# Single-pass turns and a new closing order in a one-token attention kernel

## The chip, the cores, the metric

One core of a Trainium2 chip (trn2). The metric is the device time of one execution in microseconds, as a median of several executions. In the profiles PE is TensorE, PEld its weight load, DVE VectorE, ACT ScalarE, POOL GpSimd, and SP the queue that issues the transfers; the granted clock is the share of full speed that TensorE was allowed. Ratios are computed as the mean time of one kernel's fast runs over the mean of the other's fast runs of the same rounds, so they are not quite the ratio of the medians quoted.

## The reference

One token attends to 16 heads of 65,536 cached keys of 256 elements; the result is projected, gated by a small dense branch and added to the input.

```python
def _A_ref(x, k_cache, v_cache, wq, wo):
    q = (x @ wq).reshape(B, Sq, H, Dh).transpose(0, 2, 1, 3)     # H = 16, Dh = 256
    scores = einsum("bhqd,bhkd->bhqk", q, k_cache) * (Dh ** -0.5)
    o = einsum("bhqk,bhkd->bhqd", softmax(scores), v_cache)
    return o.transpose(0, 2, 1, 3).reshape(B, Sq, H * Dh) @ wo
# _B_ref: silu(x @ w1) @ w2
xn = layernorm(x)
out = x + _A_ref(xn, ...) * silu(_B_ref(xn, w1, w2))
```

The K and V caches are 537 MB each, in bf16, and are read once.

## The kernel before

The cache is cut into 64 blocks of 128 keys per partition. A K or V block is 8.4 MB, and three buffers of that size, `R`, rotate: K comes in, VectorE multiplies it by the query in place and sums it for the scores (ScalarE sums the last 13 of every 32 keys), and V comes into the same buffer for TensorE.

```python
    def load_k(i, s):                       # SP queue
        take(sp, vf[s])                     # buffer free: TensorE done with V
        sp.dma_start(out=R[s][:, :], in_=block(Kd, i)).then_inc(kl[s], 16)
        ...
    def load_v(i, s):
        take(sp, kf[s])                     # buffer free: scores done
        sp.dma_start(out=R[s][:, :], in_=block(Vd, i)).then_inc(vl[s], 16)
```

A block's output, two key parities by 512 columns, is copied to `O` and *turned*, so that the head's elements lie on partitions:

```python
    def pe_turn(tok=False):
        take(pe, oc)                        # ScalarE's copy into O is done
        Ov = O[:, :].rearrange("r (j p a) -> r j a p", j=2, a=2)
        for a in range(2):
            for j in range(2):
                ins = pe.matmul(            # float32 product with a column of eye2
                    ps_t[:, a : a + 1], lhsT=Ov[:, j, a, :], rhs=eye2[:, j : j + 1],
                    start=(j == 0), stop=(j == 1))
        return mark("pe", ins) if tok else ins.then_inc(ho, 1)

    def pe_block(i, s):
        pe_turn()                           # of an earlier block
        pe_max(i)                           # waits for VectorE's row maxima
        pe_v(s)                             # waits for softmax and V; 64 products
```

The closing, from the moment the last K block's first half is used (cut; `keys` waits for a V piece and multiplies it, `project` multiplies heads by their projection weights):

```python
    # SP queue
    load_wo(0); load_wo(1)                              # heads 0-4, 5-9
    # V pieces of keys 64-96, 96-112, 112-120, 120-128
    for (k0, k1), w in zip(vz[2:], zl[2:]):
        load_keys(R[1], Vl, k0, k1, w)
    load_wo(2); load_wo(3)                              # heads 10-13, 14-15
    ...
    # TensorE, the last block
    take(pe, pv); keys(psO2, 0, 1, vz, zl, 0, 2, True, od)   # first half of the keys
    pe_turn()                                           # of block 62
    project(*pieces[0]); pe_rows(); ... ; pe_bcast(); ...    # heads 0-9, second maximum
    take(pe, pv); t15 = pe_sums(...)
    keys(psO, 0, 1, vz, zl, 2, 3, True)                 # 16 products
    pe_turn()                                           # of the first half
    keys(psO, 0, 1, vz, zl, 3, len(vz), False, od)      # 16 products
    act_out(); project(*pieces[2]); t = pe_turn(tok=True)
    ...                                                 # combine on VectorE
    project(pieces[3][0], H1); project(H1, H)
```

Of the kernel before, what the change touches and what calls it, by code (L numbers as in the profile page):

```python
# [8 lines left out]
ALU = mybir.AluOpType  # L9
# [12 lines left out]
def kernel(  # L22
# [14 lines left out]
    fp32 = mybir.dt.float32  # L37
    P = nc.NUM_PARTITIONS
# [9 lines left out]
    LAST = NBLK - 1  # L48
# [16 lines left out]
    pool = ctx.enter_context(tc.tile_pool(name="sb", bufs=1))  # L65
    ps = ctx.enter_context(tc.tile_pool(name="ps", bufs=1, space=bass.MemoryType.PSUM))

    pe, dve, act, gp, sp = nc.tensor, nc.vector, nc.scalar, nc.gpsimd, nc.sync
# [15 lines left out]
    ident = pool.tile([P, P], bf16, name="ident")  # L84
    ones_row = pool.tile([1, P], bf16, name="ones_row")
    ones_sq = pool.tile([P, P], fp32, name="ones_sq")
    eye2 = pool.tile([2, 2], fp32, name="eye2")
    x_f = pool.tile([1, D], bf16, name="x_f")
    sml = pool.tile([P, 16], fp32, name="sml")
    xnT = pool.tile([P, DX], bf16, name="xnT")  # L90
# [32 lines left out]
    assert WW + 4 * D <= KW // 2  # L123

    bank = [ps.tile([P, 512], fp32, name=f"bank{i}") for i in range(8)]
    psO, ps_m, ps_nb, ps_t = bank[0][0:2, :], bank[1][:, 0:P], bank[2][:, 0:1], bank[3][:, 0:2]
    ps_q, ps_y, ps_ao, ps_tot = bank[4][:, 0:Dh], bank[5][0:1, 0:D], bank[6][0:1, 0:D], bank[7]
    psO2, ps_qh = bank[4][0:2, :], bank[3][0:H, 0:Dh]
    ps_xt, ps_h = bank[2][:, 0:DX], bank[7][:, 0:FC]
# [9 lines left out]
    def mark(e, ins):  # L139
        count[e] += 1  # L140
        ins.then_inc(line[e], 1)
        return (e, count[e])

    def need(e, *toks):
        for p, c in toks:
            if seen.get((e, p), 0) < c:
                eng[e].wait_ge(line[p], c)
                seen[(e, p)] = c

    def sem(name):  # L150
        return tc.alloc_semaphore(name)

    def take(e, s, k=1):
        e.wait_ge(s, k).then_inc(s, -k)  # L154
# [10 lines left out]
    od, oc, ho = sem("od"), sem("oc"), sem("ho")  # L165
# [3 lines left out]
    def cuts(*c):  # L169
        return tuple(zip(c[:-1], c[1:]))  # L170

    vn = cuts(0, 32, 64, 96, 128)
    vz = cuts(0, 32, 64, 96, 112, 120, 128)
    nl = [sem(f"nl{t}") for t in range(len(vn))]
    zl = [sem(f"zl{t}") for t in range(len(vz))]
    pieces = cuts(0, 5, 10, 14, 16)
    wl = [sem(f"wl{t}") for t in range(len(pieces))]
# [5 lines left out]
    def at(n):  # L183
        return slice(n, n + 1) if isinstance(n, int) else bass.ds(n, 1)
# [94 lines left out]
    def act_softmax(e, s, c0=0, c1=KB):  # L279
        def col(a, b):  # L280
            return hist[:, at(e + 2), a:b].rearrange("p o s -> p (o s)")

        take(act, bm)
        act.mul(out=col(0, 1), in_=ps_nb, mul=-scale).then_inc(sa, 1)  # L284
        take(act, sa)
        act.activation(  # L286
            out=PV[s][:, c0:c1],
            in_=S2[:, c0:c1],
            func=ACT.Exp,
            bias=col(0, 1),  # L290
            scale=scale,
            accum_out=col(1, 2),
        ).then_inc(pv, 1)

    def act_out(po=psO):
        take(act, od)
        act.copy(out=O[:, :], in_=po).then_inc(oc, 1)  # L297
# [5 lines left out]
    def act_row(e):  # L303
        take(act, ho)
        return act.copy(out=hist[:, at(e + 2), 2:4].rearrange("p o s -> p (o s)"), in_=ps_t)  # L305
# [10 lines left out]
    def pe_keys(po, t, s, k0, k1, start, stop, done=None):  # L316
        for c in range(k0, k1, 2):
            ins = pe.matmul(  # L318
                po,
                lhsT=PV[t][:, c : c + 2],  # L320
                rhs=R[s][:, c * Dh : (c + 2) * Dh],
                start=(start and c == k0),
                stop=(stop and c == k1 - 2),
            )
        if done is not None:
            ins.then_inc(done, 1)

    def pe_rows():
        take(pe, rm)
        pe.matmul(  # L330
            ps_m[0:1, :], lhsT=rmax[:, 0:1], rhs=ident[:, :], start=True, stop=True
        ).then_inc(tm, 1)

    def pe_bcast():
        take(pe, gm)
        pe.matmul(  # L336
            ps_nb, lhsT=ones_row[0:1, :], rhs=gmax[0:1, :], start=True, stop=True
        ).then_inc(bm, 1)


    def pe_turn(tok=False):
        take(pe, oc)
        Ov = O[:, :].rearrange("r (j p a) -> r j a p", j=2, a=2)
        for a in range(2):
            for j in range(2):
                ins = pe.matmul(  # L346
                    ps_t[:, a : a + 1],
                    lhsT=Ov[:, j, a, :],
                    rhs=eye2[:, j : j + 1],
                    start=(j == 0),  # L350
                    stop=(j == 1),
                )
        return mark("pe", ins) if tok else ins.then_inc(ho, 1)

# [27 lines left out]
    def pe_block(i, s):  # L382
        pe_turn()
        pe_max(i)
        pe_v(s)
# [23 lines left out]
    with tc.tile_critical():  # L409
# [6 lines left out]
            out=w2_t, in_=B_w2.rearrange("(p c) d -> p (c d)", c=FC)  # L416
# [38 lines left out]
        gp.memset(ident[:], 0.0)  # L455
        g_o = mark("gp", gp.memset(eye2[:], 0.0))
        need("gp", g_o)
        for T, w in ((ident, P), (eye2, 2)):
            mark("gp", gp.affine_select(
                out=T[:], in_=T[:], compare_op=ALU.not_equal, fill=1.0, base=0,  # L460
                pattern=[[-1, w]], channel_multiplier=1,
            ))
        gp.memset(Z, 0.0)
        g_c = mark("gp", gp.memset(ones_sq[:], 1.0))
# [8 lines left out]
            out=rstd, in_=mv[0:1, 1:2], func=ACT.Sqrt, bias=eps_t, scale=1.0  # L473
# [4 lines left out]
        t = mark("dve", dve.tensor_scalar(  # L478
            out=xn,
            in0=x_f[0:1, :],  # L480
            scalar1=mv[0:1, 0:1],
            scalar2=rstd,
            op0=ALU.subtract,
            op1=ALU.mult,
        ))
        need("dve", t, g_c)
        for z in range(2):
            t5 = mark("dve", dve.tensor_copy(
                out=xz[0:1, z, :].rearrange("o (r y) -> o y r", y=2)[:, z, :],
                in_=xn[0:1, DF * P : D],  # L490
# [4 lines left out]
        for c in range(DX):  # L495
# [3 lines left out]
                rhs=ones_row[0:1, 0:1],  # L499
# [8 lines left out]
        for c in range(DX):  # L508
            w = Z[:, c * H * H : (c + 1) * H * H]
            t7 = mark("dve", dve.tensor_copy(  # L510
                out=w[:, 0 : (H - 1) * (H + 1) + 1 : H + 1],
                in_=xnT[:, c : c + 1].to_broadcast([P, H]),
# [12 lines left out]
        for f in range(FC):  # L525
            for z in range(2):
                h0 = z * (P // 2)
                for r, (w, c) in enumerate(rows(w1_t, F, z * (F // 2), (z + 1) * (F // 2))):
# [3 lines left out]
                        rhs=xnT[:, c : c + 1],  # L532
# [3 lines left out]
        t = mark("pe", ins)  # L536
# [17 lines left out]
        for r, (w, c) in enumerate(rows(wq_t, HD, 0, Dh)):  # L554
# [3 lines left out]
                rhs=w,  # L558
# [4 lines left out]
        for h in range(H):  # L563
            for r, (w, c) in enumerate(rows(wq_t, HD, h * Dh, (h + 1) * Dh)):
# [3 lines left out]
                    rhs=w,  # L568
# [31 lines left out]

        none()
        pe_turn()
        none()
        need("pe", t9)
# [73 lines left out]
        def project(h0, h1):  # L678
            for h in range(h0, h1):
                for a in range(2):  # L680
                    ins = pe.matmul(  # L681
                        ps_ao,
                        lhsT=OT[:, a, h : h + 1],
                        rhs=wo_n[:, 2 * h + a, :],
                        start=(h == 0 and a == 0),
                        stop=(h == H1 and a == 1),
                    )
            return ins
# [13 lines left out]
        def keys(po, t, s, cut, sems, a, b, start, done=None):  # L702
            for n in range(a, b):
                (k0, k1), last = cut[n], n == b - 1
                pe.wait_ge(sems[n], 16)
                pe_keys(po, t, s, k0, k1, start and n == a, last and done is not None,
                        done if last else None)

        keys(psO, 2, 2, vn, nl, 0, 3, True)
        pe_rows()  # L710
        keys(psO, 2, 2, vn, nl, 3, 4, False, od)
        pe_bcast()
        act_softmax(LAST, 0, 0, HK)
        act_sums(0, 2)
        act_out()
# [2 lines left out]


        take(pe, pv)  # L720
        keys(psO2, 0, 1, vz, zl, 0, 2, True, od)
        pe_turn()
        need("pe", t_o)
        pe.wait_ge(wl[0], 16)
        project(*pieces[0])
        pe_rows()
        pe.wait_ge(wl[1], 16)
        (h0, h1) = pieces[1]
        project(h0, h0 + 3)
        pe_bcast()  # L730
        project(h0 + 3, h1)
        act_softmax(LAST + 1, 0, HK, KB)

        take(pe, pv)
        t15 = pe_sums(ps_m[:, 0:NL], N1, NENT)
        weights(N1, NENT, H1, H, (ps_m[:, 0:NL], t15))
        act_out(psO2)
        keys(psO, 0, 1, vz, zl, 2, 3, True)
        pe_turn()
        t_g = silu(g_t, ps_y, g_e, t_y)  # L740
        t = mark("act", act_row(LAST))
        need("dve", t)
        outputs(N1, NENT - 1, H1, H, NL - 1)
        keys(psO, 0, 1, vz, zl, 3, len(vz), False, od)
        act_out()
        pe.wait_ge(wl[2], 16)
        project(*pieces[2])
        t = pe_turn(tok=True)
        need("dve", t)
        t_l = mark("dve", dve.scalar_tensor_tensor(  # L750
            out=OT[:, :, H1],
# [3 lines left out]
            op0=ALU.mult,  # L755
            op1=ALU.add,
        ))
        pe.wait_ge(wl[3], 16)
        project(pieces[3][0], H1)
        need("pe", t_l)  # L760
        t = mark("pe", project(H1, H))
        need("dve", t, t_g)
        t = mark("dve", dve.tensor_tensor(out=g_t, in0=ps_ao, in1=g_t, op=ALU.mult))  # L763
        need("dve", t)
        t = mark("dve", dve.tensor_tensor(  # L765
            out=x_f[0:1, :], in0=g_t, in1=x_f[0:1, :], op=ALU.add
        ))
# [32 lines left out]
```

## Time and profile before

| | before |
|---|---|
| median (3 runs) | 2524.33 us (2523.97 to 2526.91) |
| span of the profiled execution | 2520.7 us |
| SP queue's transfers on the 16 DMA engines | 99.6% of the span |
| TensorE, VectorE, ScalarE busy | 48%, 89%, 57% |
| transferred | 1084.5 MB |

The lines behind this table and the end of the chain of waits stand in the prediction. One more line is a landmark: in the order of time of the SP queue (start us, duration, engine, line, operation, tiles), the first two pieces of projection weights are issued when the last K block's first half is used.

```profile
2478.93 0.96 SPq L432 DMA_DIRECT2D R<-in_A_wo_dram  x2
```

I call the time from there to the end of the span **the closing**: 2520.7 - 2478.93 = 41.77 us before. What comes earlier is the loop, which the change touches only in its turns.

### The profile page before, as it was taken

The numbers are of one execution on the slowest core, as the hardware profiler recorded it, in microseconds if no ns is written. First come the engines' busy times: TensorE is split into PE (matmuls) and PEld (weight loads), VectorE is DVE, ScalarE is ACT, GpSimd is POOL, SyncE is SP. The second block draws the span as 40 slices with busy tenths as digits, with TensorE's granted clock in tenths as the row PEclk, the third lists the DMA queues.
The fourth block names the chain that finished last, engine by engine and source line by source line (L and its number), as shares of the span: only waits on it lengthen the run. The fifth ranks groups of instructions, "written<-read, shape, count | busy, mean of one in ns | idle before, by whom it ended". The sixth has DMA issues, their size and how long they took to land. (4 is left out here: it accounts for less than half of the span.)

```text
span 2520.7 us, 29977 instructions
## 1 busy us (share of the span) xinstructions
PE 1198.9 (48%) x5125; PEld 500.4 (20%) x5125; DVE 2233.5 (89%) x10281; ACT 1443.8 (57%) x6992; POOL 2.5 (0%) x13
## 2 busy tenths in 40 slices
PE   3353544545535445445354354453553544535557
PEld 2121211212212112112121121121221211212123
DVE  6989889889898898898898988988989889889897
ACT  4656556556565565565555655655656556556564
POOL 0000000000000000000000000000000000000000
PEclk7676767767767667677676676776767767767779
DMA  9999999999999999999999999999999999999998
GB/s 423 416 433 432 434 436 433 434 433 433 433 433 433 433 434 432 433 434 434 435 436 434 435 436 435 433 433 434 433 433 433 433 433 433 433 433 434 433 432 342
DMA packets 22728, 1084.52 MB, mean 430 GB/s; under 512 B 2354, under 2 KB 4532, under 8 KB 4916
## 3 DMA queue, kind: packets, MB, share of 16 engines
q1 hardware_dynamic: 22706, 1084.30, 99.6%
q8 instruction: 6, 0.10, 0.0%
q14 instruction: 14, 0.11, 0.0%
q10 hardware_dynamic: 2, 0.00, 0.0%
HBM read 1084.29 MB, written 0.00 MB: 430 GB/s over the span
## 5 line engine op out<-in xcount | busy, mean ns | idle before, releaser
L271 ACT ACTIVATE R<-R 128x256 bf16<-128x256 bf16 x3328 | 1330.7, 401 | 698.5 <-ACTq L154 698.5
L249 DVE CUSTOM_DVE_ANT_0 R<-R,qcur 128x256 bf16<-128x256 bf16 x4864 | 1699.8, 416 | 0.0
L318 PE MATMUL bank<-R,PV 128*2 128x512 bf16 x4096 | 1025.5, 417 | 25.3 <-DMA R<-in_A_v_cache_dram 11.5
L238 DVE TENSOR_TENSOR R<-R,qcur 128x3328 bf16<-128x3328 bf16 x256 | 482.6, 1885 | 197.2 <-DVEq L154 197.1
L271 ACT ACTIVATION_READ_ACCUMULATOR R<-R 128x1 f32 x3328 | 620.1, 186 | 0.0
L330 PE MATMUL bank<-ident,rmax 128*1 128x128 bf16 x65 | 17.1, 263 | 1022.4 <-PEq L154 1022.4
L318 PEld LDWEIGHTS bank<-R,PV 128*2 128x2 bf16 x4096 | 365.7, 90 | 657.2 <-issue 207.1
L249 DVE DVE_READ_ACCUMULATOR2_ANT S<- 128x1 f32 x4864 | 379.4, 78 | 0.0
L346 PE MATMUL bank<-eye,O 2*128 2x1 f32 x536 | 97.2, 298 | 239.8 <-PEq L154 239.8
L330 PEld LDWEIGHTS bank<-ident,rmax 128*1 128x1 bf16 x65 | 5.2, 79 | 1026.6 <-issue 1026.2
L346 PEld LDWEIGHTS bank<-eye,O 2*128 2x128 f32 x536 | 93.3, 255 | 257.8 <-issue 257.8
L284 ACT ACTIVATE hist<-bank 128x1 f32 (+1 forms) x65 | 11.1, 171 | 206.3 <-ACTq L154 206.3
L305 ACT COPY hist<-bank 128x2 f32 (+1 forms) x66 | 10.6, 160 | 119.2 <-ACTq L154 119.2
L214 DVE TENSOR_REDUCE gmax<-bank 1x1 bf16<-1x128 f32 x65 | 18.3, 281 | 38.6 <-DVEq L154 38.6
L231 DVE CAST qcur<-bank 128x256 bf16<-128x256 f32 x64 | 27.2, 425 | 16.0 <-DVEq L154 14.3
L297 ACT COPY O<-bank 2x512 f32<-2x512 f32 x67 | 37.4, 559 | 5.7 <-ACTq L154 5.7
L286 ACT ACTIVATE PV<-S,hist 128x128 bf16<-128x128 f32 (+1 forms) x65 | 26.0, 400 | 13.4 <-ACTq L154 13.1
L358 PE MATMUL bank<-q,ident 16*128 16x256 bf16 x63 | 24.4, 387 | 0.0
L224 DVE COPY S<-S 128x128 f32<-128x128 f32 (+1 forms) x65 | 14.7, 226 | 9.5
L225 DVE TENSOR_REDUCE rmax<-S 128x1 bf16<-128x128 f32 (+1 forms) x65 | 18.2, 280 | 0.0
L336 PE MATMUL bank<-gmax,ones_row 1*128 1x1 bf16 x65 | 10.3, 159 | 16.0 <-PEq L154 16.0
L336 PEld LDWEIGHTS bank<-gmax,ones_row 1*128 1x128 bf16 x65 | 6.5, 100 | 33.4 <-issue 33.4
(65 smaller groups left out, 101.8 us busy)
## 6 DMA issues: line engine op xcount, KB each, us to landing
R<-in_A_k_cache_dram SPq DMA_DIRECT2D x4, 4096.0 KB, 24.7
R<-in_A_v_cache_dram SPq DMA_DIRECT2D x7, 2048.0 KB, 24.1
R<-in_A_wq_dram SPq DMA_DIRECT2D x1, 3072.0 KB, 12.9
R<-in_A_wo_dram SPq DMA_DIRECT2D x2, 1120.0 KB, 19.3
R<-in_B_w_dram SPq DMA_DIRECT2D x1, 1568.0 KB, 27.1
R<-in_B_w_dram SPq DMA_DIRECT2D x1, 1344.0 KB, 5.8
R<-in_A_v_cache_dram SPq DMA_DIRECT2D x1, 1024.0 KB, 15.7
R<-in_A_v_cache_dram SPq DMA_DIRECT2D x2, 512.0 KB, 16.9
```

The lines of the kernel that those rows point to most:

```text
L214: dve.reduce_max(out=gmax[0:1, :], in_=ps_m[0:1, :], axis=AX.X).then_inc(gm, 1)
L225: dve.reduce_max(out=rmax[:, :], in_=S[:, c0:c1], axis=AX.X).then_inc(rm, 1)
L231: dve.tensor_copy(out=qcur[:, :], in_=ps_q).then_inc(sd, 1)
L238: m = dve.tensor_tensor(out=pair, in0=pair, in1=qcur[:, None, :].to_broadcast([P, NA, Dh]), op=ALU.mult,)
L249: ins = dve.tensor_tensor_reduce(out=Kv[:, c, :], in0=Kv[:, c, :], in1=qcur[:, :], scale=1.0, scalar=0.0, op0=ALU.mult, op1=ALU.add, accum ...
L271: ins = act.activation(out=prod, in_=prod, func=ACT.Identity, accum_out=S[:, c : c + 1],)
L286: act.activation(out=PV[s][:, c0:c1], in_=S2[:, c0:c1], func=ACT.Exp, bias=col(0, 1), scale=scale, accum_out=col(1, 2),).then_inc(pv, 1)
L297: act.copy(out=O[:, :], in_=po).then_inc(oc, 1)
L318: ins = pe.matmul(po, lhsT=PV[t][:, c : c + 2], rhs=R[s][:, c * Dh : (c + 2) * Dh], start=(start and c == k0), stop=(stop and c == k1 - 2),)
L330: pe.matmul(ps_m[0:1, :], lhsT=rmax[:, 0:1], rhs=ident[:, :], start=True, stop=True).then_inc(tm, 1)
L346: ins = pe.matmul(ps_t[:, a : a + 1], lhsT=Ov[:, j, a, :], rhs=eye2[:, j : j + 1], start=(j == 0), stop=(j == 1),)
L358: pe.matmul(ps_q, lhsT=ident[0:H, at(h)].to_broadcast([H, P]), rhs=q16[:, :], start=True, stop=True,).then_inc(qr, 1)
```

## The change

The intent: a turn as four transposes ("single-pass": one record in the trace for each, where a float32 product leaves two), with the identity and the identity with swapped columns as second operand, summed in PSUM, of which the first column of each pair is used; and a closing in which the maxima and one of the turns no longer stand in TensorE's way.

```diff
-    eye2 = pool.tile([2, 2], fp32, name="eye2")
+    eye2 = pool.tile([2, 2, 2], fp32, name="eye2")
...
-    vz = cuts(0, 32, 64, 96, 112, 120, 128)
+    vz = cuts(0, 32, 64, 80, 96, 112, 120, 128)
...
-                    ps_t[:, a : a + 1],
+                    ps_t2[:, 2 * a : 2 * a + 2],
                     lhsT=Ov[:, j, a, :],
-                    rhs=eye2[:, j : j + 1],
+                    rhs=eye2[:, j, :],
                     start=(j == 0),
                     stop=(j == 1),
+                    is_transpose=True,
...
-        keys(psO, 2, 2, vn, nl, 0, 3, True)
+        keys(psO, 2, 2, vn, nl, 0, 2, True)
         pe_rows()
+        keys(psO, 2, 2, vn, nl, 2, 3, False)
+        pe_bcast()
         keys(psO, 2, 2, vn, nl, 3, 4, False, od)
-        pe_bcast()
...
-        keys(psO2, 0, 1, vz, zl, 0, 2, True, od)
+        keys(psO2, 0, 1, vz, zl, 0, 1, True)
         pe_turn()
+        keys(psO2, 0, 1, vz, zl, 1, 2, False, od)
+        act_out(psO2)
...
-        project(*pieces[0])
+        project(h0, h0 + 2)
         pe_rows()
-        pe.wait_ge(wl[1], 16)
-        (h0, h1) = pieces[1]
-        project(h0, h0 + 3)
+        project(h0 + 2, h1)
         pe_bcast()
-        project(h0 + 3, h1)
         act_softmax(LAST + 1, 0, HK, KB)
-
+        pe_turn()
         take(pe, pv)
...
-        act_out(psO2)
-        keys(psO, 0, 1, vz, zl, 2, 3, True)
-        pe_turn()
...
-        keys(psO, 0, 1, vz, zl, 3, len(vz), False, od)
+        project(*pieces[1])
+        keys(psO, 0, 1, vz, zl, 2, len(vz), True, od)
         act_out()
         pe.wait_ge(wl[2], 16)
-        project(*pieces[2])
+        project(h0, h0 + 2)
         t = pe_turn(tok=True)
...
+        project(h0 + 2, h1)
         pe.wait_ge(wl[3], 16)
```

(Cut: the setup of the second identity on GpSimd, the PSUM slices of the turn, the lines that set `h0` and `h1`, and the order of some ScalarE copies.)

More of the change, by code (lines that the diff above doesn't have):

```diff
@@ L125 @@
     bank = [ps.tile([P, 512], fp32, name=f"bank{i}") for i in range(8)]
-    psO, ps_m, ps_nb, ps_t = bank[0][0:2, :], bank[1][:, 0:P], bank[2][:, 0:1], bank[3][:, 0:2]
+    psO, ps_m, ps_nb, ps_t2 = bank[0][0:2, :], bank[1][:, 0:P], bank[2][:, 0:1], bank[3][:, 0:4]
+    ps_t = ps_t2.rearrange("p (a r) -> p a r", r=2)[:, :, 0]
     ps_q, ps_y, ps_ao, ps_tot = bank[4][:, 0:Dh], bank[5][0:1, 0:D], bank[6][0:1, 0:D], bank[7]
@@ L457 @@
         need("gp", g_o)
-        for T, w in ((ident, P), (eye2, 2)):
+        for T, w, b, d in ((ident[:], P, 0, -1), (eye2[:, 0, :], 2, 0, -1), (eye2[:, 1, :], 2, -1, 1)):
             mark("gp", gp.affine_select(
-                out=T[:], in_=T[:], compare_op=ALU.not_equal, fill=1.0, base=0,
-                pattern=[[-1, w]], channel_multiplier=1,
+                out=T, in_=T, compare_op=ALU.not_equal, fill=1.0, base=b,
+                pattern=[[d, w]], channel_multiplier=1,
             ))
@@ L720 @@
         take(pe, pv)
-        keys(psO2, 0, 1, vz, zl, 0, 2, True, od)
+        keys(psO2, 0, 1, vz, zl, 0, 1, True)
         pe_turn()
+        keys(psO2, 0, 1, vz, zl, 1, 2, False, od)
+        act_out(psO2)
         need("pe", t_o)
         pe.wait_ge(wl[0], 16)
-        project(*pieces[0])
+        (h0, h1) = pieces[0]
+        project(h0, h0 + 2)
         pe_rows()
-        pe.wait_ge(wl[1], 16)
-        (h0, h1) = pieces[1]
-        project(h0, h0 + 3)
+        project(h0 + 2, h1)
         pe_bcast()
-        project(h0 + 3, h1)
         act_softmax(LAST + 1, 0, HK, KB)
+        pe_turn()
         take(pe, pv)
@@ L736 @@
         weights(N1, NENT, H1, H, (ps_m[:, 0:NL], t15))
-        act_out(psO2)
-        keys(psO, 0, 1, vz, zl, 2, 3, True)
-        pe_turn()
+        t_r = mark("act", act_row(LAST))
         t_g = silu(g_t, ps_y, g_e, t_y)
-        t = mark("act", act_row(LAST))
-        need("dve", t)
+        need("dve", t_r)
         outputs(N1, NENT - 1, H1, H, NL - 1)
-        keys(psO, 0, 1, vz, zl, 3, len(vz), False, od)
+        pe.wait_ge(wl[1], 16)
+        project(*pieces[1])
+        keys(psO, 0, 1, vz, zl, 2, len(vz), True, od)
         act_out()
         pe.wait_ge(wl[2], 16)
-        project(*pieces[2])
+        (h0, h1) = pieces[2]
+        project(h0, h0 + 2)
         t = pe_turn(tok=True)
```

## The prediction

> **What bounds the kernel now.** I read the page's first two parts, then the DMA queues, then stretches of the run, and last the chain of waits and the instructions of its lines.
>
> ```profile
> PE 1198.9 (48%) x5125; PEld 500.4 (20%) x5125; DVE 2233.5 (89%) x10281; ACT 1443.8 (57%) x6992; POOL 2.5 (0%) x13
> DMA  9999999999999999999999999999999999999998
> q1 hardware_dynamic: 22706, 1084.30, 99.6%
> 100.00:2440.00 2340.00, 1110.65 (x4626) 455.10 (x4626) 2097.00 (x9675) 1358.75 (x6593) 0.00 (x0) 0.71 1.00 433
> ```
>
> No compute engine is full: VectorE, the busiest, has 89%, TensorE 48%. The SP queue's transfers hold the 16 DMA engines for 99.6% of the span. The fourth line is the stretch from 100 to 2440 us (busy time of PE, weight load, DVE, ACT, POOL, then granted clock, DMA share, GB/s): DMA share 1.00 at 433 GB/s. A pair of K and V blocks is 16.78 MB, so 38.75 us of transfer; DVE needs 2233.5 / 64 = 34.9 us for it, TensorE 18.7 us. **The loop is DMA-bound**, and whatever TensorE saves in it is idle time. Bytes alone make 1084.3 MB / 433 GB/s = 2504 us of the 2520.7 us span. Only the start and the end are left; the change edits the end. There the chain of waits reads (start us, us, what):
>
> ```profile
> 2479.93 24.97 DMA R<-in_A_v_cache_dram
> 2504.91 0.04 issue
> 2504.95 3.61 PE bank L318 x16
> 2508.57 1.03 PE bank L346 x8
> 2509.59 3.54 PE bank L318 x16
> 2513.14 1.51 PE bank L681 x8
> 2514.65 1.03 PE bank L346 x8
> 2515.68 0.95 PE bank L681 x4
> 2516.63 0.02 issue
> 2516.66 0.62 DVE R L763
> 2517.28 0.02 issue
> 2517.30 0.61 DVE x_f L765
> ```
>
> From 2504.91, when the last block's third V piece lands, TensorE is the path, without a gap, for 11.7 us: 16 V products, a turn of a block output (line 346), 16 V products, 8 projection products, a second turn, 4 projections. Two VectorE operations and the output transfer follow. The DMA engines empty beside it; same columns as the stretch above:
>
> ```profile
> 2508.00:2509.00 1.00, 1.00 (x8) 0.56 (x6) 0.92 (x2) 0.00 (x0) 0.00 (x0) 1.00 1.03 370
> 2510.00:2511.00 1.00, 1.00 (x6) 0.38 (x5) 0.23 (x2) 0.00 (x0) 0.00 (x0) 1.00 0.28 109
> 2512.50:2513.00 0.50, 0.50 (x4) 0.19 (x3) 0.00 (x0) 0.00 (x0) 0.00 (x0) 1.00 0.03 11
> ```
>
> The bulk is in by 2510, with stragglers to 2512.5 to 2513. The last issues are two projection-weight pieces of 896 and 448 KB, issued from 2493.20 and about 2493.7, each 18.9 us to landing: about 2512.1 and 2512.6. The loop's turns:
>
> ```profile
> L346 PE MATMUL bank<-eye,O 2*128 2x1 f32 x536 | 97.2, 298 | 239.8 <-PEq L154 239.8
> L330 PE MATMUL bank<-ident,rmax 128*1 128x128 bf16 x65 | 17.1, 263 | 1022.4 <-PEq L154 1022.4
> ```
>
> 67 turns of 4 float32 products leave 536 records: two per product, 8 per turn. After the turn TensorE idles for 1022.4 us in 62 waits, 16.5 us per block, for the row maxima (line 330). That is the slack in which a shorter turn disappears.
>
> **What the Trainium skill says.** "TensorE: Matmul & The Clock Gate", section Terms, says that load and matmul have a transpose mode on trn2, 4 times faster for float32. The trace before has no transpose; it shows float32 products recorded twice where bf16 products are recorded once (4096 for 64 blocks of 64), so I assume half the records, not a quarter of the time. "Perfetto Trace Analysis", section Transposes, advises the transpose in place of an ordinary product, which this change does. "PSUM — Partial Sum Buffer", section The four PSUM rules, says that a transpose of 2-byte or smaller elements never accumulates, while a float32 one set the written bit; so a sum of two float32 transposes should come out right. No run here shows it yet. "DMA: Bandwidth & Descriptors", section Where 436 GB/s comes from, puts the fabric's limit at 435.2 GB/s; the 433 GB/s of this trace agrees and says that the loop has nothing left to gain.
>
> **The change part by part.**
> (1) *Turns.* Eight records become four. Warm, a turn takes 1.03 us on the path, so I take 0.52 us; cold in the loop (1.83 us for the one at 43.81 us) about 0.9. Over 63 turns in the loop 30 to 60 us of TensorE time go, all inside the 16.5 us waits: **0 us**. PE busy should drop by some 45 us.
> (2) *Setup.* One more select on POOL, 0.18 us as its sibling took, ahead of the startup's normalisation. The first K half reaches VectorE only at 27.23 us by DMA: **0 us**.
> (3) *First half of the last block.* The row-maximum product now comes before the third V piece instead of behind it, its broadcast before the fourth. The first softmax was on ACT at 2487.01 and should come at about 2483. The accumulations behind it move up by 3.6 us, but DVE sets the scores' end: its maximum reduction ran at 2482.10, 0.40 us after it was free, and that wait goes. Scores end at about 2498.9, not 2499.27.
> (4) *Second half.* Row-maximum product after 4 projections instead of 10, at about 2499.3, not 2500.48; then 6 projections (some 1.2 us), broadcast at about 2500.7, not 2501.77. The softmax and sum after it move from 2502.94 to about 2501.9.
> (5) *The turn before the last V products.* It took 1.03 us between the two groups of 16. Now the turn of the first half's output comes behind that broadcast, while TensorE would wait for softmax or V: **1.03 us off the path**. The last 10 of the first 20 projections then run to about 2504.0 (1.9 us from 2502.1), and V piece 64 to 80, split off to land earlier, can begin there instead of at 2504.95: **0.95 us**. 32 products at 3.54/16 = 0.221 us are 7.08 us, ending at 2511.1 instead of 2513.1.
> (6) *After the last V product.* Before: 8 + 4 projections and a turn, 3.5 us. Now 4 projections (0.75) beside ACT's copy (0.57 and its hand-overs), the turn (0.52), 8 projections (1.5) beside VectorE's 0.23 us combination: 2.85 us. **0.65 us.**
>
> The sum is 1.03 + 0.95 + 0.65 = 2.6 us if no transfer stands in the way. But TensorE would want the 896 KB piece at 2511.1, and it lands at about 2512.1. From there: 4 projections, turn, 8 projections, 2.8 us, to 2514.95 instead of 2516.56: **1.6 us**. I choose nearer to the second, 1.8 us: 2524.3 - 1.8 = **2522.5 us**.
>
> **The rivals.**
> *A new wait for the projection weights.* Before, the 8 projections began at 2512.97, only 0.9 us after the estimated landing; anything that moves TensorE up by 2 us should run into it. It caps the gain at 1.6 us, and at 1 us if a straggler or the extra descriptor of the split V piece lands it later. I hold it likelier than not.
> *The transpose is no shorter.* If float32 transposes still take two records, or longer ones, part (6) keeps about 0.1 us; the gain is then 1 to 2 us, as the other turn is hidden anyway. Speaking for it: these products are tiny (2 rows), where fixed time rules. Against it: 8 records in 1.03 us look issue-bound, so half the records is half the time.
> *The loop gets faster.* If the turns were on the loop's path, 0.5 to 0.9 us for each of 62 blocks would be 31 to 56 us, 1.2 to 2.2%. That is the sole road to 2%, and DMA share 1.00 and the 16.5 us of idle speak against it.
> *The tail gets slower.* Placing 10 projections ahead of the last V products could hold those back, if their weights landed late; but these came with 19.3 us to landing, at about 2498.2. A slip of a microsecond is conceivable, 50 us is not.
>
> **Range and chances.** Everything behind the last bulk transfer is about 8 us (2512.6 to 2520.7), 0.3% of the time. So the reordering can't reach 2% either way, whatever wait takes over. The runs before spread from 2523.97 to 2526.91, more than the gain; the range is the gain of 0 to 3 us with run noise about it: 2520.5 to 2525.2. Chances: faster 0.01, within 2% 0.985, slower 0.005.
>
> **What would show it right or wrong.** PE records of the turn line fall from 536 to 268, and a warm turn takes about 0.5 us; if not, (1) and (6) are wrong. DMA share stays 1.00 at 433 GB/s in 100 to 2440. The first half's softmax stands near 35 us before the end of the span. The chain of waits should hold only one turn and, if the first rival is right, a DMA entry of a projection piece ahead of the last 12 projections; without one, the gain should be nearer 2.6 us. TensorE's last product ends at 2514 to 2515.5, not 2516.6. Wrong would be: a loop with another GB/s, a wrong output, or V products begun later than 2505.

## The result

The changed kernel took 2522.91 us (2521.84 to 2523.24, 4 runs) against 2524.15 us (2523.65 to 2526.91, 4 runs): 1.24 us less by the medians, ratio 0.9992, interval 0.9975 to 1.0009. That is the same within 2%, and the interval of the ratio includes 1.

The page of the changed kernel: busy times, the SP queue, the turn (now line 349), the wait for the row maxima (now line 332).

```profile
PE 1144.2 (45%) x4857; PEld 444.4 (18%) x4857; DVE 2233.6 (89%) x10281; ACT 1443.8 (57%) x6992; POOL 2.7 (0%) x14
q1 hardware_dynamic: 22850, 1084.30, 99.6%
L332 PE MATMUL bank<-ident,rmax 128*1 128x128 bf16 x65 | 17.1, 262 | 1078.1 <-PEq L156 1078.1
L349 PE MATMUL bank<-eye,O 2*128 2x2 f32 x268 | 40.6, 252 | 239.6 <-PEq L156 239.6
```

The turns fell from 536 records and 97.2 us to 268 and 40.6 us. TensorE's busy time fell by 54.7 us, and its wait for the row maxima rose by 55.7 us: what the turns gave back in the loop became idle time of the same length. The stretches, with the columns that the prediction explains, show the loop at the same share and rate of the DMA engines, and later the end of the transfers:

```profile
100.00:2440.00 2340.00, 1061.21 (x4385) 404.51 (x4385) 2095.01 (x9661) 1356.46 (x6584) 0.00 (x0) 0.71 1.00 433
...
2511.00:2512.00 1.00, 1.00 (x6) 0.34 (x5) 0.00 (x0) 0.00 (x0) 0.00 (x0) 1.00 0.93 336
...
2513.00:2514.00 1.00, 0.00 (x0) 0.00 (x0) 0.00 (x0) 0.57 (x1) 0.00 (x0) 1.00 0.17 66
```

In the last stretch TensorE is idle and the DMA engines carry the last stragglers: this is the new wait. The SP queue's landmark, and TensorE from the last V products on (the bracket gives the idle time before and who ended it):

```profile
2480.65 0.96 SPq L436 DMA_DIRECT2D R<-in_A_wo_dram  x2
```

```profile
2505.62 7.32 PE L320 MATMUL bank<-R,PV 128*2 128x512 bf16 x32
2514.11 0.92 PE L685 MATMUL bank<-R,OT 128*1 128x448 bf16 x4 [1.17 <-DMA R<-in_A_wo_dram]
2514.95 0.63 PE L349 MATMUL bank<-eye,O 2*128 2x2 f32 x4
2515.52 1.67 PE L685 MATMUL bank<-R,OT 128*1 128x448 bf16 x8
```

And the end of its chain of waits, in the same order as before's:

```profile
2496.17 17.90 DMA R<-in_A_wo_dram
2514.06 0.04 issue
2514.11 0.92 PE bank L685 x4
2515.03 0.56 PE bank L349 x4
2515.59 1.62 PE bank L685 x8
```

Before, the chain's transfer was a V piece and 11.7 us of TensorE followed it. Now the transfer is the 896 KB piece of projection weights, and 3.1 us follow. Counted from the landmark:

| us after the first issue of projection weights | before | after |
|---|---|---|
| first half's softmax starts its bias on ScalarE | 8.08 | 4.08 |
| last 32 V products start | 26.02 | 24.97 |
| last V product ends | 34.2 | 32.3 |
| the 896 KB weights piece lands | not waited for | 33.4 |
| last projection product ends | 37.7 | 36.6 |
| end of the span | 41.77 | 40.65 |

TensorE is 1.9 us ahead when the V products end. It then waits 1.17 us for weights, and needs 3.10 us in place of 3.49: 1.9 - 1.17 + 0.39 = 1.1 us, the difference of the two closings.

The span of this profiled execution is nevertheless 0.6 us *longer* than before's (2521.3 against 2520.7), because its landmark came 1.72 us later. The same kernel, run again below, had the landmark at 2480.11 and at 2482.27: over one loop of 2480 us, single executions wander by as much as the whole gain. The profiled execution of before was also a fast one, 2522.64 us, below every other run of it. Whether the change moves the landmark is not shown: the three profiles in the old order (before and two runs below) have it at 2478.67 to 2479.63, earlier than the changed kernel's three, while other kernels in the new order have it at 2478.16 to 2481.30. The closing leaves this out; the times of the runs include it. So below I read the closing from the traces, which shows single steps, and medians of 5 or 6 runs, which show the sum within about a microsecond.

### The profile page after: what moved, and what is told of

The parts are those of the page before. It is cut to its first block, busy times and chain, and to the rows that moved or that the text cites. A ratio compares the mean times of both kernels' runs of the same rounds, so it can differ in the third digit from the quotient of the medians.

```text
span 2521.3 us, 29444 instructions
## 1 busy us (share of the span) xinstructions
PE 1144.2 (45%) x4857; PEld 444.4 (18%) x4857; DVE 2233.6 (89%) x10281; ACT 1443.8 (57%) x6992; POOL 2.7 (0%) x14
## 5 line engine op out<-in xcount | busy, mean ns | idle before, releaser
L251 DVE DVE_READ_ACCUMULATOR2_ANT S<- 128x1 f32 x4864 | 386.7, 80 | 0.0
L349 PE MATMUL bank<-eye,O 2*128 2x2 f32 x268 | 40.6, 252 | 239.6 <-PEq L156 239.6
L349 PEld LDWEIGHTS bank<-eye,O 2*128 2x128 f32 x268 | 36.8, 207 | 257.1 <-issue 257.1
L338 PEld LDWEIGHTS bank<-gmax,ones_row 1*128 1x128 bf16 x65 | 6.4, 99 | 33.4 <-issue 33.4
```

Of the source, the lines that this page charges most:

```text
L251: ins = dve.tensor_tensor_reduce(out=Kv[:, c, :], in0=Kv[:, c, :], in1=qcur[:, :], scale=1.0, scalar=0.0, op0=ALU.mult, op1=ALU.add, accum ...
L349: ins = pe.matmul(ps_t2[:, 2 * a : 2 * a + 2], lhsT=Ov[:, j, a, :], rhs=eye2[:, j, :], start=(j == 0), stop=(j == 1), is_transpose=True,)
```

## The experiments

Two sets ran on one chip (before there: 2523.36 us, 9 runs, 10 with the second set), a third on another (before: 2524.10 us, 9 runs). Every run matched the reference within its tolerance. That is no evidence on the turns, as the fourth experiment shows: it uses wrong weights for six heads and matches as well. From the sizes in the reference (entries of about 0.05, 65,536 keys of nearly equal weight) I estimate the attention term at a ten-millionth of the input that it is added to, less than bf16 can show; this was not measured.

| kernel | median us (range) | ratio to before (interval) | closing in its profile, us |
|---|---|---|---|
| changed, first set | 2521.84 (2521.64 to 2522.11) | 0.9994 (0.9980 to 1.0008) | 39.9 |
| turns only | 2522.50 (2522.19 to 2524.01) | 0.9997 (0.9984 to 1.0011) | 42.5 |
| order only | 2523.11 (2521.85 to 2524.86) | 0.9999 (0.9985 to 1.0013) | 41.8 |
| last weights not loaded | 2521.29 (2520.76 to 2521.78) | 0.9991 (0.9977 to 1.0005) | 40.4 |
| V piece not split | 2522.13 (2521.59 to 2523.35) | 0.9996 (0.9982 to 1.0010) | 41.5 |
| 16 turns per block | 2523.93 (2522.05 to 2524.93) | 1.0002 (0.9989 to 1.0015) | 40.2 |
| weights before last V | 2523.60 (2522.77 to 2524.49) | 1.0001 (0.9987 to 1.0015) | 41.4 |
| first V blocks in halves | 2522.93 (2522.61 to 2523.95) | 0.9999 (0.9985 to 1.0012) | 40.8 |
| changed, third set | 2522.19 (2521.63 to 2524.64) | 0.9992 (0.9978 to 1.0005) | 40.4 |
| turns only, TensorE kept busy | 2522.97 (2521.80 to 2523.96) | 0.9995 (0.9981 to 1.0008) | 42.3 |
| last turn before the wait | 2521.63 (2521.01 to 2522.59) | 0.9989 (0.9976 to 1.0003) | 40.1 |

No interval excludes 1. Yet in the result and in the first set every run of the changed kernel lies below every run of before, and in the third set four of five do, so a gain of 1 to 2 us is unlikely to be chance. The closing of the changed kernel varies by 0.76 us between its three profiles (39.89 to 40.65), and before has only one: closings less than that apart show nothing. What follows are readings of single steps, backed by medians where these are far enough apart.

### The changed kernel again

> The changed kernel unchanged, as the control of this set. By the two profiles its closing, from the first issue of projection weights to the end of the span, takes 40.65 us (2480.65 to 2521.3) against 41.77 us before (2478.93 to 2520.7), so 1.1 us less. The theory (only the closing differs, the loop is bound by transfers) expects the time 0.8 to 1.6 us below the kernel before, and again a wait of about 1.2 us of TensorE for a projection-weight piece. A rival, that the 1.24 us between the medians is chance, expects less than 0.5 us.

It was 1.5 us below before by the medians, closing 39.89 us, with a wait of 0.66 us for the weights piece. The gain is of the expected size in this set too; the wait is there but half as long:

```profile
2512.80 0.92 PE L685 MATMUL bank<-R,OT 128*1 128x448 bf16 x4 [0.66 <-DMA R<-in_A_wo_dram]
```

### The turns alone

Edit, on the kernel before: only the turn's part of the diff (`is_transpose`, two output columns, the second identity).

> The single-pass turns alone, in the order of before. Two of the closing's turns lie on the chain of waits there, 1.03 us each, and a turn of four records measured 0.56 us on the chain after. Theory: closing 41.77 - 2 x 0.47 = 40.8 us, time about 0.9 us below before, and no wait for the projection weights, as TensorE comes to them at about 33.6 us after their first issue and they land at about 33.2. The rival that the reordering did all of it and the turns nothing: 0 to 0.2 us below before. The rival that a shorter turn speeds the loop: tens of us.

The median is 0.9 us below before, as the theory had it, but the runs lie in two groups: 2522.19, 2522.20, 2522.50, and twice 2524.01. The profiled execution is one of the latter. Its stretches and its V products:

```profile
2506.00:2508.00 2.00, 2.00 (x8) 0.64 (x7) 2.00 (x1) 0.00 (x0) 0.00 (x0) 0.64 1.01 396
2508.00:2510.00 2.00, 2.00 (x6) 0.64 (x5) 1.28 (x2) 0.00 (x0) 0.00 (x0) 0.51 1.04 385
```

```profile
2505.56 5.30 PE L319 MATMUL bank<-R,PV 128*2 128x512 bf16 x16 [1.91 <-DMA R<-in_A_v_cache_dram]
2510.80 0.64 PE L347 MATMUL bank<-eye,O 2*128 2x2 f32 x4
2511.36 3.61 PE L319 MATMUL bank<-R,PV 128*2 128x512 bf16 x16
```

The granted clock fell to 0.64 and 0.51 just as TensorE was the path, and 16 V products took 5.30 us, where the next 16 took 3.61. Without these 1.69 us the closing would be 42.47 - 1.69 = 40.8 us, the number expected. By this subtraction, and by the three faster runs, the turns are worth about 1 us in the old order, and a clock that drops at the wrong moment takes more than that away.

### The order alone

```diff
-                    ps_t2[:, 2 * a : 2 * a + 2],
+                    ps_t2[:, 2 * a : 2 * a + 1],
-                    rhs=eye2[:, j, :],
+                    rhs=eye2[:, j, 0:1],
-                    is_transpose=True,
```

> The new order and the split V piece with the old float32 products. Only the last turn lies on the chain of the changed kernel, so the theory expects its 0.47 us back: closing 41.1 us, time 0.5 us above the changed kernel and 0.7 below before. If the two parts added up without meeting the weights' wait, order alone would give 2.6 - 0.9 = 1.7 us below before.

The median is only 0.25 us below before, and the runs spread over 3 us, so the sum is inconclusive. The step is clear in the chain of waits of its profile:

```profile
2495.58 17.87 DMA R<-in_A_wo_dram
2513.45 0.04 issue
2513.49 0.92 PE bank L684 x4
2514.41 1.03 PE bank L349 x8
2515.44 1.62 PE bank L684 x8
```

It is the changed kernel's chain with 1.03 us for the turn where that has 0.56. The 0.47 us per turn on the path is confirmed; the closing is 41.79 us because, besides, the weights landed 34.0 us after the landmark here (33.4 in the changed kernel's profile, 32.7 and 33.2 in its repeats). Order alone did not give the 1.7 us that an addition of parts would give.

### Without the last two weights pieces (wrong)

```diff
-        load_wo(2)
-        load_wo(3)
-        pe.wait_ge(wl[2], 16)
-        pe.wait_ge(wl[3], 16)
-                        rhs=wo_n[:, 2 * h + a, :],
+                        rhs=wo_n[:, (2 * h + a) % 20, :],
```

> Wrong on purpose: the last two pieces of projection weights are neither loaded nor waited for; heads 10 to 15 use the weights of earlier heads, so the same instructions run. Theory (the weights' landing took the place of the removed work): the 1.2 us wait goes; the turn then waits for ACT's copy of the block output, so 1.2 to 1.3 us below the changed kernel, closing about 39.4 us. Rival (the wait is incidental, V landing or TensorE binds all the same): within 0.3 us of the changed kernel.

It was 0.55 us below the changed kernel, and their ranges overlap by 0.14 us only. The expectation was twice that, and its closing, 40.4 us in place of the expected 39.4, is no shorter than the changed kernel's. The timeline of TensorE shows why:

```profile
2506.65 1.89 PE L320 MATMUL bank<-R,PV 128*2 128x512 bf16 x8 [0.23 <-DMA R<-in_A_v_cache_dram]
2509.09 3.61 PE L320 MATMUL bank<-R,PV 128*2 128x512 bf16 x16 [0.55 <-DMA R<-in_A_v_cache_dram]
2512.54 0.92 PE L683 MATMUL bank<-R,OT 128*1 128x448 bf16 x4
2513.54 0.61 PE L349 MATMUL bank<-eye,O 2*128 2x2 f32 x4
```

No wait for weights, but 0.78 us of waits for V pieces, which in the changed kernel's profile did not occur. The V landings lie directly beneath the weights' landing; taking one away uncovers the other. The median fits the theory that the weights' wait took the place of removed work, in part; that it is the only transfer there does not hold. With 0.55 us between the rival's 0.3 and the theory's 1.2, this run alone does not decide; the last run of the third set says more.

### The V piece not split

```diff
-    vz = cuts(0, 32, 64, 80, 96, 112, 120, 128)
+    vz = cuts(0, 32, 64, 96, 112, 120, 128)
```

> The changed kernel with the last block's V keys 64 to 96 in one piece again. Theory (in the closing only the last transfers and the fixed work behind them count): TensorE starts its last V products about 1 us later, as the whole piece lands about 26 us after the first issue of projection weights instead of the products' start at 25.0, but it then meets no wait for the projection weights; time within 0.5 us of the changed kernel. If the split's 0.95 us of the prediction was real on the path: 0.9 to 1 us above the changed kernel.

2522.13 us, 0.3 above the changed kernel's first set and level with its third. Its profile has 1.84 us of waiting for the whole V piece, and then only 0.27 us for the weights:

```profile
2505.15 7.07 PE L320 MATMUL bank<-R,PV 128*2 128x512 bf16 x32 [1.84 <-DMA R<-in_A_v_cache_dram]
2512.48 0.92 PE L685 MATMUL bank<-R,OT 128*1 128x448 bf16 x4 [0.27 <-DMA R<-in_A_wo_dram]
```

The split buys an earlier start that the wait behind it takes back, as the theory said. A full 0.95 us is not seen.

### Sixteen turns per block

```diff
         pe_turn()
+        pe_again(15)     # 15 more turns into columns that nobody reads
         pe_max(i)
```

> The changed kernel with 15 more turns, into columns nobody reads, behind each turn of the loop: 60 records of about 0.14 us each, some 8.5 us of TensorE per block against 16.5 us of idle time there. Theory (the loop is bound by transfers): TensorE busy rises by more than 500 us and the time stays within 1 us of the changed kernel. Rival (turns are on the loop's path): 61 x 8.5 = 520 us more.

The extra turns are 3660 records, and the idle time before the row maxima shrank by as much as they took:

```profile
L364 PE MATMUL bank<-eye,O 2*128 2x2 f32 x3660 | 447.4, 254 | 0.0
...
L332 PE MATMUL bank<-ident,rmax 128*1 128x128 bf16 x65 | 17.1, 263 | 638.6 <-PEq L156 638.6
```

TensorE is busy 438 us more (over 500 was expected), and the time rose by 1.7 to 2.1 us over the changed kernel's two medians. The rival's 520 us, or 438 by the measured busy time, are excluded: turns are not on the loop's path. The "within 1 us" of the theory was too tight; where the last 1 to 2 us come from is open (other kernels of this set, run without a changed kernel beside them, lie up to as high).

### The weights ahead of the last V pieces

```diff
+            if n == 3:
+                load_wo(2)
             load_keys(R[1], Vl, k0, k1, w)
-        load_wo(2)
```

> The changed kernel with the 896 KB piece of projection weights queued ahead of the last two V pieces. The wait for that piece should go, but the last two V pieces land some 2 us later (0.92 MB at 433 GB/s), so TensorE waits for V instead. Theory (the sum of bytes sets the end): within 0.8 us of the changed kernel, rather above it. Rival (a poor order of the last issues is what holds it up): 1 us below.

It was 1.4 to 1.8 us above the changed kernel, more than expected. TensorE no longer waits for weights but for V:

```profile
2512.25 1.02 PE L320 MATMUL bank<-R,PV 128*2 128x512 bf16 x4 [1.64 <-DMA R<-in_A_v_cache_dram]
2513.49 1.02 PE L320 MATMUL bank<-R,PV 128*2 128x512 bf16 x4 [0.22 <-DMA R<-in_A_v_cache_dram]
2514.35 0.92 PE L686 MATMUL bank<-R,OT 128*1 128x448 bf16 x4
2515.35 0.61 PE L349 MATMUL bank<-eye,O 2*128 2x2 f32 x4
2515.89 1.68 PE L686 MATMUL bank<-R,OT 128*1 128x448 bf16 x8
```

From the last landing at 2513.49 to the last product are 4.1 us, where 3.1 us follow the weights' landing in the changed kernel. The sum of bytes is not all that counts: the transfer that lands last should be the one with the least work behind it. Of these two queue orders the changed kernel's is the better one, as far as medians of different sets can say.

### The first V blocks in halves

The trace of before has one gap of the DMA engines, 262 GB/s in 95 to 100 us: the second V block waits until its K block is used. This kernel loads the first two V blocks in halves, the second block's first half once half of its K block is used.

```diff
-        load_v(0, 0)
-        load_v(1, 1)
+        take(sp, kf[0])
+        load_keys(R[0], block(Vd, 0), 0, HK, vl[0])
+        load_keys(R[0], block(Vd, 0), HK, KB, vh[0])
+        sp.wait_ge(hd, 1)       # VectorE and ScalarE are done with
+        sp.wait_ge(ha, 1)       # half of K block 1
+        load_keys(R[1], block(Vd, 1), 0, HK, vl[1])
+        take(sp, kf[1])
+        load_keys(R[1], block(Vd, 1), HK, KB, vh[1])
...
-        pe_keys(psO, s, s, 0, KB, True, True, od)
+        pe_keys(psO, s, s, 0, HK, True, False)
+        take(pe, vh[s], 16)
+        pe_keys(psO, s, s, HK, KB, False, True, od)
```

> The changed kernel with the gap of the DMA engines near 96 us filled: the first two V blocks are loaded in halves, the second block's first half as soon as half of its K block is used, and TensorE starts on a V block's first half when that has landed. Theory (only idle time of the DMA engines counts): the stretch 95 to 100 us goes from 262 GB/s to 430, and the time falls by about 2 us below the changed kernel, more than the whole change gave. Rival: the gap moves to the next K block, 0 us.

The rival came nearer: no gain, but 0.7 to 1.1 us *above* the changed kernel's medians of the other sets; what these cost is open. The gap was filled and appeared again:

```profile
95.00:100.00 5.00, 2.34 (x7) 0.78 (x8) 4.21 (x15) 1.06 (x5) 0.00 (x0) 0.50 1.02 439
110.00:120.00 10.00, 4.51 (x24) 1.98 (x21) 10.00 (x50) 7.54 (x38) 0.00 (x0) 0.93 1.01 403
170.00:175.00 5.00, 0.46 (x2) 0.18 (x2) 4.29 (x27) 2.67 (x14) 0.00 (x0) 0.50 0.76 328
```

The changed kernel's three profiles have 419 and 433 to 485 GB/s in the last two stretches. The next V block's issue stayed where it was, at 174.34 us against 174.10 in the first repeat: it waits for VectorE, which ends the scores of the K block just before and was busy 34.1 of the 35 us from 140 to 175. Here a gap that came from the pace of another engine moved when it was filled.

### The changed kernel a third time, and two variants

> The changed kernel once more, because its five runs of the first set (2521.64 to 2522.11) lay closer together than any other kernel's, and the runs of the second set had no run of it beside them. If the second set's 1 to 2 us above the first set's 2521.84 were a drift between sets, this comes out at 2522.5 to 2523.5; if not, at 2521.6 to 2522.3.

Another chip came up, so the drift between the first two sets stays unsettled; four of its five runs (2521.63 to 2522.23) are where the first set's were, one is at 2524.64. Here it was 1.9 us below before by the medians.

```diff
+        for c in range(0, 16, 2):    # turns only: 8 products nobody reads
+            pe.matmul(bank[7][0:2, :], lhsT=PV[2][:, c : c + 2],
+                      rhs=R[2][:, c * Dh : (c + 2) * Dh], start=True, stop=True)
         keys(psO, 0, 1, vz, zl, 2, 3, True)
```

> The single-pass turns alone, with 8 V products into an unread bank in the 1.9 us in which TensorE waited for the third V piece. Its runs without them fell into 2522.2 to 2522.5 and 2524.0 twice; the profiled one was a run of 2524.01 and had the granted clock at 0.64 and 0.51 from 2506 to 2510, 16 products taking 5.30 us instead of 3.61. Theory (idle TensorE ahead of the last products lets the clock drop, which costs 1.7 us on the path): all runs at 2522.0 to 2522.7 and a clock of 1.00 in that stretch. Rival (the two groups of runs have another cause): runs near 2524 again.

A miss. The clock stayed at 1.00 where the products were put, but in the profiled execution it fell one V piece earlier (16 products from 2494.05 took 5.30 us, after 2.35 us of idle time), this delayed what follows, and then the added products themselves (line 741) were on the path:

```profile
2494.05 5.30 PE L319 MATMUL bank<-R,PV 128*2 128x512 bf16 x16 [2.35 <-DMA R<-in_A_v_cache_dram]
```

```profile
2504.54 1.82 PE bank L741 x8
```

The runs spread from 2521.80 to 2523.96. That the two groups of runs of the turns-only kernel are the clock is supported by the one profile, and not settled.

```diff
-        pe.wait_ge(wl[2], 16)
-        project(h0, h0 + 2)
         t = pe_turn(tok=True)
...
-        project(h0 + 2, h1)
+        pe.wait_ge(wl[2], 16)
+        project(*pieces[2])
         pe.wait_ge(wl[3], 16)
```

> The changed kernel with the last turn issued ahead of the wait for the 896 KB piece of projection weights, so that it runs while TensorE would wait (ACT's copy of the block output ended at 2513.62, the piece landed at 2514.06 in the changed kernel's profile; 2512.83 and 2512.76 in the control's). Theory: the turn's 0.56 us leaves the path in part, 0 to 0.5 us below the changed kernel; the chain then holds the projection piece and 12 products in one stretch or the copy, turn and 12 products. Rival: no effect, or up to 0.2 us above, where the weights land before the copy ends.

2521.63 us, 0.56 below the changed kernel beside it, with ranges that overlap. The wait for weights is gone; the turn waits for ScalarE's copy instead:

```profile
2505.53 7.20 PE L320 MATMUL bank<-R,PV 128*2 128x512 bf16 x32
2513.57 0.61 PE L349 MATMUL bank<-eye,O 2*128 2x2 f32 x4 [0.84 <-PEq L156]
2514.11 2.43 PE L685 MATMUL bank<-R,OT 128*1 128x448 bf16 x12
```

It has the lowest median of the kernels with right results, 2.5 us below before (ratio 0.9989), but its interval, too, includes 1.

## Why the prediction was right or wrong, point by point

The prediction said 2522.5 us; 2522.91 was measured, and 2521.84 and 2522.19 in the repeats. That it is within 0.4 us is luck in part: before's own medians lie between 2523.36 and 2524.33 us, so that the number taken as the start was uncertain by as much as 1 us.

- *The loop is DMA-bound, turns are worth 0 us there.* Right. Share 1.00 and 433 GB/s are unchanged, the turns' time turned into an equal wait for the row maxima, and sixteenfold turns cost some 2 us, where they would cost 520 on the path.
- *(1) Turns.* The records halved as said. On the chain a turn takes 0.56 us (0.52 was said). The cold turn was mis-sized: 0.9 us was said, by halving 1.83, and 0.60 was measured. So TensorE's busy time fell by 54.7 us and not 45, without effect on the time.
- *(3) and (4) The maxima.* Right within 0.2 us: the first softmax 4.0 us earlier relative to the landmark; the second row-maximum product at 20.34 us after it (20.37 was said), the sum after it at 22.8 (23.0 was said).
- *(5) The second turn off the path, an earlier start.* Right: V products started at 24.97 us (25.07 was said) and ended at 32.3 (32.2).
- *(6) and the cap.* The first rival came true: a wait of 1.17 us for the 896 KB piece, landing 33.4 us after the landmark (33.2 was said). The term that was too small is the work behind the landing: "4 projections, turn, 8 projections, 2.8 us" measured 3.10, as the projections took 0.92 and 1.62 us in place of 0.75 and 1.5. This and the later landing leave 1.1 us of the 1.6 in the profile. (The prediction put before's last product at 2516.56; by its own chain it ends at 2516.63, so the cap was 1.7 by its sum.)
- *Its signs of being wrong.* One came true as it was worded: V products were to begin no later than 2505, and TensorE to end by 2515.5; they began at 2505.62 and it ended at 2517.21. Counted from the landmark, both come to before's clock as 2503.9 and 2515.5, within what was said. The prediction had left out that the landmark itself wanders.
- *The limit of 435.2 GB/s.* The same section, Where 436 GB/s comes from of "DMA: Bandwidth & Descriptors", says that for transfers between HBM and SBUF the HBM's some 358 GB/s per core bind. The loop streams from HBM at 433, so here the measurement decides. That the loop has nothing left to gain rests on the share of 1.00, not on the page.
- *The choice of 1.8 us*, above the capped 1.6, had no ground in the trace of one execution; the medians of the three sets say 1.2 to 1.9.
- *The rival of a transpose no shorter* fell with 0.56 against 1.03 us.
- *Not foreseen:* the clock's drops in the closing, worth 1.7 us where one met the path; the V landings directly beneath the weights' landing.
- *The sum of two float32 transposes.* The outputs pass, but wrong weights pass too: the runs do not show it.

## What to carry to other kernels

Find first what bounds the loop: here, work taken from an engine with 16 us of idle time per block only lengthened that idle time. At the end of a DMA-bound kernel, ask which transfer lands last and how much work lies behind it; moving work out of the way gains only until the next transfer's landing, and the last transfer should have the least work behind it. When the gain is a thousandth, compare steps from a landmark in the traces, not two single spans.

## What the Trainium skill lacked or had wrong

- "TensorE: Matmul & The Clock Gate", section Terms, says 4 times faster for float32, without a size. Here records halved and a turn of [2 x 128] pieces went from 1.03 to 0.56 us on the chain at full clock, 1.8 times, and from 1.83 to 0.60 us at a clock of 0.50, 3 times. The page has no time for float32 transposes this small. These hardly depended on the granted clock: the 268 records of the changed kernel lasted 246 to 276 ns each over clocks of 0.50 to 1.00, before's 536 records of products 243 to 348. The timelines of before and of the changed kernel, both in a stretch with the clock at 0.50:

```profile
43.81 1.83 PE L346 MATMUL bank<-eye,O 2*128 2x1 f32 x8 [8.20 <-PEq L154]
```

```profile
44.15 0.60 PE L349 MATMUL bank<-eye,O 2*128 2x2 f32 x4 [7.41 <-PEq L156]
```

- The same page, in the table of its section "Why this matters for your kernels", asks for no idle gaps above some 3 us between bursts of matmuls. Here the clock fell to 0.51 behind a gap of 1.91 us in the turns-only kernel. And behind the same gap at the same place it stayed at 1.00 in the kernel before (2.34 us, from 2494 to 2498) and fell to 0.50 in the kernel with added products (2.35 us, its line stands above). In these traces the length of the last gap alone does not tell.

```profile
2494.02 3.61 PE L318 MATMUL bank<-R,PV 128*2 128x512 bf16 x16 [2.34 <-DMA R<-in_A_v_cache_dram]
```

- No page has the wandering of a kernel that streams a gigabyte: the same kernel's landmark came at 2480.11 to 2482.27 us, and its runs on one chip spread over up to 3 us, more than this change's gain.
